# Another hand-written order of steps in a one-core attention and feed-forward layer

## The chip, the cores and the metric

The kernel runs on one core of one Trainium2 chip. The metric is the device time of an execution in microseconds (us); less is better. Five engines matter: TensorE (PE in the profile, its weight loads PEld), VectorE (DVE), ScalarE (ACT), GpSimd (POOL), and SyncE (SP), whose queue issues nearly all DMAs here. Each engine runs its own list of instructions in order. An instruction that waits holds up all that stands behind it on its engine, and a DMA that waits for its source holds up the DMAs behind it on SP's queue.

## The reference

The input x has 2048 rows of 640. There are 32 heads of 20 columns. All inputs are bfloat16.

```python
def _A_ref(x, wqkv, w_phi, wo):
    q, k, v = qkv[0], qkv[1], qkv[2]
    pq = jnp.einsum("bhsd,hdf->bhsf", q, w_phi)
    pk = jnp.einsum("bhsd,hdf->bhsf", k, w_phi)
    phi_q = jnp.concatenate([_softmax(pq, axis=-1), _softmax(-pq, axis=-1)], axis=-1)
    phi_k = jnp.concatenate([_softmax(pk, axis=-1), _softmax(-pk, axis=-1)], axis=-1)
    kv = jnp.einsum("bhsf,bhsd->bhfd", phi_k, v)
    z  = jnp.einsum("bhsf->bhf", phi_k)
    num = jnp.einsum("bhqf,bhfd->bhqd", phi_q, kv)
    den = jnp.einsum("bhqf,bhf->bhq", phi_q, z)[..., None] + 1e-6
    o = num / den
    return (lambda x, *d: x.transpose(*d))(o, 0, 2, 1, 3).reshape(B, S, D) @ wo
...
h = x + _A_ref(_layernorm(x, axis=-1), A_wqkv, A_w_phi, A_wo)
h2 = h + _B_ref(_layernorm(h, axis=-1), B_w1, B_w2)
```

`_B_ref` is a product with w1 (640 x 1728), a SiLU, and a product with w2 (1728 x 640). The layer norm has no weights. Linear attention of this kind needs the sum over all 2048 keys before any query can be finished.

## The kernel before

The rows are cut into 16 tiles of 128 (t = 0 to 15). All work is cut into named steps, `add(name, emit)`; the string `ORDER` lists the names, and at the end of the kernel one loop runs through it and emits each step's instructions:

```python
for name in ORDER:
    steps.pop(name)()
```

No scheduler comes after that. The order of the list is the order of the instructions on each engine, and so what waits behind what. The engines run beside each other: two steps that stand side by side in the list and belong to different engines overlap, as far as their inputs allow. The dictionary `ON` names the engine of those steps that can run on more than one.

The steps, by their engine and the lines of the profile:

- **Loads** stand ahead of the list and are not part of it: on SP's queue, in this order, X's first row tile (L165), five blocks of Wk (L168), X tile 1, Wv (L178), X tiles 2 and 3, Wq (L180), X tiles 4 to 7, X tiles 8 to 15. `load0` to `load11` in the list are the loads of wo (0), w1 (1 to 5), w2 (6 to 9) and the last rows of w2 (10 and 11), all on SP (L421).
- **Folding.** The products with w_phi are folded into the weights once: `wk0..4` transpose Wk on PE (L306), `wke` copies the result from PSUM (L323), `fk` multiplies it with phi on PE (L333), and `fk..e` copies it to Wfk (L342). For the queries `wq0..4` transposes Wq by DMA on SP into WTq (L325, one block each), `fq` multiplies on PE (L333), `fq..e` copies (L342). `warm` steps are matmuls on constants, `phi_a` and `phi_b` set up the folded factor on VectorE.
- **Normalising a tile:** `st` the moments on VectorE (L373, L374), `rs` the inverse deviation (on ScalarE by a logarithm and an exponential, L379 and L380; on POOL by an addition and a power, L382 and L385), `xn` the normalised row (L389, VectorE or POOL), `xt` its transposition (tiles 0 to 3 on PE, L396, with a copy `x` from PSUM, L416; the others by DMA on SP, L418).
- **Keys and values:** `K` and `V` project on PE (L429), `ex` takes the exponentials on ScalarE (L461), `su` sums them on VectorE (L465), `rk` inverts the sums on ScalarE (L473, L474), `sc` scales on VectorE (L478), `ve` copies the values on ScalarE (L482), and `kv` adds the tile into the key-value sums on PE (L497).
- **Queries:** `Q` projects on PE (L444), `qe` exponentials on ScalarE (L557), `qs` sums and `qr` ratios on VectorE (L561, L569 to L579), `qt` transposes by DMA on SP (L585).
- **Attention:** after `kv15`, `bd0` and `bd1` on VectorE mask the sums into KVB (L506, L508). `D` multiplies on PE (L610), `E` divides on VectorE (L622, L623), `ot` transposes by DMA (L634), `G` is the product with wo on PE (L643), `ga` adds the residual on VectorE (L650).
- **Feed-forward:** `ls`, `lr`, `hn`, `ht` normalise and transpose again (VectorE, POOL, VectorE, SP L670). From there tiles 0 and 1 stand alone and the others go in pairs: `u2.4` is the product with w1 of the pair that begins with tile 2, block 4 (L733; `.L` the last half block, L744), `s` its SiLU on ScalarE (L753), `lt` the transposition of the last half block (L763), `d` the product with w2 on PE (L771), `oa` the last addition on VectorE (L780) and `out` the store on SP (L785).

Two kinds of buffers tie the steps together. PSUM has eight banks: up to the step `halves` they are three pairs that go round in the order of the PE steps that take one (two more banks hold the key-value sums), after it eight single banks that go round. A PE step waits until the step that read the bank's last content is done. In SBUF there are four buffers each for the normalised rows, the key exponentials and the values, three for the transposed queries.

Of the kernel before, what the change touches and what calls it, by code (L numbers as in the profile page):

```python
# [34 lines left out]
s0.L ga20 lr1 lt0 u0.4 s0.0 hn1 qr4 G21 ht1 s0.4 u0.8 ga21 ls2 u0.12 s0.8 G30 s0.12 lr2 G31 ga30 d00
hn2 ga31 ht2 ls3 qt4 u1.L qs5 lr3 u1.0 s1.L d01 hn3 s1.0 oa00 ht3 qr5 lt1 u1.4 oa01 qs6 qt5 u1.8
s1.4 qr6 u1.12 s1.8 out0 u2.L D4 s1.12 u2.0 qs7 s2.L lt2 d10 s2.0 qs8 qt6 E40 u2.2 E41 d11 s2.2 oa10
ot4 qr7 D5 oa11 u2.4 qs9 u2.6 s2.4 E50 u2.8 s2.6 E51 ot5 u2.10 s2.8 u2.12 qt7 s2.10 D6 s2.12 G40 E60
G41 E61 d20 ga40 ot6 ga41 ls4 out1 lr4 hn4 ht4 G50 G51 d21 ga50 oa20 ga51 ls5 d30 lr5 hn5 d31 qr8
# [5 lines left out]
ga91 out5 ls9 ht8 d70 qr13 lr9 hn9 d71 oa61 ht9 out6 qt13 G100 G101 ga100 oa70 D11 oa71 u8.L u8.0
ga101 s8.L E110 u8.2 E111 s8.0 qs14 ot11 u8.4 s8.2 lt8 u8.6 qr14 s8.4 u8.8 ls10 qt14 s8.6 u8.10 lr10
s8.8 out7 hn10 u8.12 s8.10 qs15 ht10 s8.12 G110 G111 ga110 D12 d80 E120 ga111 E121 d81 ls11 ot12
oa80 lr11 d90 hn11 oa81 ht11 qr15 d91 oa90 G120 G121 ga120 oa91 u10.L D13 s10.L u10.0 lt10 E130 E131
u10.2 s10.0 ga121 ot13 ls12 u10.4 s10.2 lr12 u10.6 s10.4 hn12 u10.8 s10.6 ht12 u10.10 s10.8 out8
out9 qt15 u10.12 s10.10 D14 s10.12 G130 G131 ga130 d100 ga131 ls13 E140 lr13 d101 hn13 oa100 ht13  # L50
# [104 lines left out]

# [692 lines left out]
```

## Time and profile before

| | us |
|---|---|
| median of 3 runs | 237.06 (236.93 to 239.13) |
| span of the profiled execution, first to last instruction | 235.7 |
| time around that span: median less span | 1.4 |
| PE busy | 230.5 (98%) |
| VectorE busy | 170.0 (72%) |
| ScalarE busy | 107.8 (46%) |
| POOL busy | 46.7 (20%) |

The profiled execution has no other time of its own than the span. A sum made against the trace is made against the 235.7 us; the measured times are 1.4 us above it.

The profile shows one execution. In a timeline a line has the start, the duration, the engine, the kernel's line, the operation with its output and inputs, and in brackets how long the engine sat idle before it and what ended that. Several instructions of one line that follow each other are merged (x3). Durations of matmuls overlap; from start to start is what counts. A list of waits has the engine and line that waited, what it waited for, the total in us, how often, and the longest. A DMA's line on SP's queue is its issue; it lands later, and the landing times are given apart.

The slices of the span show at which time which engine is full: VectorE is at 9 tenths or more in most slices up to a third of the span and below that afterwards, ScalarE has work up to about 90 us, and POOL mostly up to 54 us.

### The profile page before, as it was taken

The numbers are of one execution on the slowest core, as the hardware profiler recorded it, in microseconds if no ns is written. First come the engines' busy times: TensorE is split into PE (matmuls) and PEld (weight loads), VectorE is DVE, ScalarE is ACT, GpSimd is POOL, SyncE is SP. The second block draws the span as 40 slices with busy tenths as digits, with TensorE's granted clock in tenths as the row PEclk, the third lists the DMA queues.
The fourth block names the chain that finished last, engine by engine and source line by source line (L and its number), as shares of the span: only waits on it lengthen the run. The fifth ranks groups of instructions, "written<-read, shape, count | busy, mean of one in ns | idle before, by whom it ended". The sixth has DMA issues, their size and how long they took to land.

```text
span 235.7 us, 5600 instructions
## 1 busy us (share of the span) xinstructions
PE 230.5 (98%) x2256; PEld 181.4 (77%) x2256; DVE 170.0 (72%) x355; ACT 107.8 (46%) x230; POOL 46.7 (20%) x80
## 2 busy tenths in 40 slices
PE   8899999999999999999999999999999999999995
PEld 6677777777777779798877878877877977877874
DVE  4699999899999758899669787696885544463021
ACT  3788997997888777231401501400510420421500
POOL 3117778990000011200020110011001100010000
PEclk9999999999999999999999999999999999999999
DMA  6996858499452842864431695617445193222001
GB/s 167 328 389 129 103 141 170 128 202 281 101 108 64 209 88 52 107 143 92 89 86 28 139 165 116 123 32 136 85 108 55 33 147 83 31 61 61 3 29 56
DMA packets 66697, 27.50 MB, mean 117 GB/s; under 512 B 58992, under 2 KB 65648, under 8 KB 66544
## 3 DMA queue, kind: packets, MB, share of 16 engines
q1 hardware_dynamic: 66016, 27.13, 53.2%
q8 instruction: 17, 0.28, 0.5%
q10 hardware_dynamic: 656, 0.03, 0.2%
q14 instruction: 8, 0.07, 0.1%
HBM read 10.43 MB, written 2.62 MB: 55 GB/s over the span
## 4 chain that ended last, share of the span: by engine, by line
PE 90%; DMA 6%; SPq 2%; issue 0%; DVE 0%; DVEq 0%
PE banks L733 24%; PE banks L771 24%; PE banks L429 15%; PE banks L444 9%; PE banks L643 9%; DMA Wq<-in_A_wqkv_dram 4%; DMA WTq<-Wq 3%; PE banks L497 2%; PE banks L610 2%; PE banks L774 2%; PE banks L744 1%; PE banks L333 1%; SPq L168 1%; SPq L165 1%; SPq L178 0%
## 5 line engine op out<-in xcount | busy, mean ns | idle before, releaser
L771 PE MATMUL banks<-w_sb,shT 128*128 128x320 bf16 (+2 forms) x429 | 61.3, 295 | 0.0
L733 PE MATMUL banks<-HnT,w_sb 128*128 128x256 bf16 (+1 forms) x585 | 60.0, 261 | 0.0
L733 PEld LDWEIGHTS <-w_sb 128*128 128x128 bf16 x585 | 51.3, 98 | 5.4
L771 PEld LDWEIGHTS <-shT 128*128 128x128 bf16 x429 | 41.1, 98 | 15.0
L753 ACT ACTIVATE shT<-banks 128x512 bf16<-128x512 f32 (+2 forms) x57 | 31.4, 559 | 36.0 <-PE banks L733 34.6
L429 PEld LDWEIGHTS <-XnT 128*128 128x128 bf16 x320 | 30.3, 98 | 12.0 <-issue 1.1
L382 POOL TENSOR_SCALAR rs<-mv 128x1 f32<-128x1 f32 x22 | 5.0, 227 | 159.9 <-DVE mv L374 159.8
L373 DVE BATCH_NORM_STATS2 st<-X 128x6 f32<-128x320 bf16 x64 | 27.9, 477 | 4.6 <-DMA X<-in_A_x_dram 4.5
L759 ACT ACTIVATE sh_l<-banks 128x128 bf16<-128x128 f32 x9 | 2.5, 278 | 62.4 <-PE banks L744 50.8
L780 DVE TENSOR_TENSOR o_t<-banks,X 128x320 bf16<-128x320 f32 (+2 forms) x33 | 15.5, 476 | 19.2 <-PE banks L774 19.2
L650 DVE TENSOR_TENSOR X<-banks,X 128x320 bf16<-128x320 f32 x32 | 15.3, 484 | 15.2 <-PE banks L643 15.0
L643 PE MATMUL banks<-wo_sb,OT 128*128 128x320 bf16 x160 | 25.1, 299 | 0.0
L429 PE MATMUL banks<-Wv,XnT 128*128 128x320 bf16 x160 | 23.8, 299 | 1.0 <-DMA Wv<-in_A_wqkv_dram 1.0
L557 ACT ACTIVATE EQ<-banks 128x660 bf16<-128x660 f32 (+2 forms) x48 | 21.8, 541 | 5.2 <-PE banks L444 5.0
L561 DVE TENSOR_REDUCE Sq<-EQ 128x66 f32<-128x1320 bf16 x16 | 24.2, 1516 | 0.0
L429 PE MATMUL banks<-Wfk,XnT 128*128 128x320 bf16 x160 | 24.0, 299 | 0.0
L444 PE MATMUL banks<-Wfq,XnT 128*128 128x360 bf16 (+2 forms) x160 | 23.3, 300 | 0.0
L465 DVE TENSOR_REDUCE Sk<-EK 128x64 f32<-128x1280 bf16 x16 | 23.3, 1465 | 0.0
L389 POOL TENSOR_SCALAR xn<-X,mv,rs 128x640 bf16<-128x640 bf16 x9 | 22.6, 2508 | 3.3 <-ACT rs L380 3.0
L461 ACT ACTIVATE EK<-banks 128x640 bf16<-128x640 f32 x32 | 20.7, 699 | 1.5 <-PE banks L429 1.4
L444 PEld LDWEIGHTS <-XnT 128*128 128x128 bf16 x160 | 15.4, 97 | 6.4
L643 PEld LDWEIGHTS <-OT 128*128 128x128 bf16 x160 | 15.2, 98 | 5.1
(63 smaller groups left out, 208.3 us busy)
## 6 DMA issues: line engine op xcount, KB each, us to landing
...
X<-in_A_x_dram SPq DMA_DIRECT2D x1, 1280.0 KB, 13.4
...
```

Source lines behind the costliest of these rows:

```text
L373: nc.vector.bn_stats(st[:, i, :], X[:, t, i * HD : (i + 1) * HD])
L389: eng.tensor_scalar(out=xn_[t][:], in0=X[:, t, :], scalar1=mv_.pop(t)[:, 0:1], scalar2=rs_.pop(t)[:], op0=ALU.subtract, op1=ALU.mult,)
L429: nc.tensor.matmul(ps[:, g, 0:HD], XnT[:, c, t * P : (t + 1) * P], W[:, c, g * HD : (g + 1) * HD], start=(c == 0), stop=(c == C - 1),)
L444: nc.tensor.matmul(ps[:, 0 : e - a], XnT[:, c, t * P : (t + 1) * P], Wfq[:, c, a:e], start=(c == 0), stop=(c == C - 1),)
L461: nc.scalar.activation(E5[:, :, :, b, :], p4, AF.Exp, scale=sign)
L465: nc.vector.tensor_reduce(sk[t][:], ek[t][:, 0 : H * HF].rearrange("p (q f) -> p q f", f=DH), axis=AX.X, op=ALU.add)
L557: nc.scalar.activation(features(t, a, b)[:, :, :, i], p4, AF.Exp, scale=sign)
L561: nc.vector.tensor_reduce(sq[t][:], EQ[0][:, t, :, 0:FCH].rearrange("p c (q f) -> p c q f", f=DH), axis=AX.X, op=ALU.add)
L643: nc.tensor.matmul(ps[:, 0:HD], ot[t][:, c, :], wo_sb[:, c, g * HD : (g + 1) * HD], start=(c == 0), stop=(c == C - 1),)
L733: nc.tensor.matmul(ps[:, at : at + n], w1_sb[:, c, fc * P : fc * P + P], HnT[u][:, c, 0:n], start=(c == 0), stop=(c == C - 1),)
L753: nc.scalar.activation(shT[u][:, f0 * n : f1 * n], ps_of.pop(("u", u, f0))[:, 0 : (f1 - f0) * n], AF.Silu)
L771: nc.tensor.matmul(ps[:, 0 : b - a], shT[u][:, at : at + P], w2_sb[:, fc, a:b], start=(fc == 0), stop=False,)
```

## The change

The list `ORDER` is replaced by another one with the same steps. The two are alike only at the end, from `d120` on. The order of the tiles stays, but which step of one kind stands beside which of another changes nearly everywhere: the warm matmuls all come first, the DMA transposes of Wq come in another order (`wq3 wq0 load10 wq1 wq4 load3 xt4 wq2` on SP, instead of `wq0 wq1 wq2 xt4 wq3 xt5 wq4`), the weight loads stand elsewhere, the Q steps lie differently between the key steps, and the blocks of a feed-forward pair are computed in another sequence.

`ON` moves some steps: the normalised rows on VectorE are now those of tiles 0, 2, 4, 9, 11, 12 and 14 (before: 0, 1, 2, 3, 4, 6 and 12), the other nine stay on POOL or go there; the inverse deviations on ScalarE are now those of tiles 0, 5, 7 and 14 (before ten: 0, 2, 3, 7, 8, 9, 10, 12, 14 and 15), the others are on POOL; the copy `wke3` goes from ScalarE to VectorE. What each step computes is unchanged.

```diff
--- before.py
+++ after.py
@@ -16,44 +16,42 @@
 ORDER = """
-warm5 warm2 warm15 warm7 warm20 warm13 warm0 warm16 warm18 ones2 warm9 warm8 ones3 warm6 st0 warm10
-ones1 warm12 warm19 warm17 phi_b warm21 rs0 warm1 phi_a warm4 warm3 wk0 xn0 warm11 warm14 wke0 wk1
-xt0 wk2 wke1 wk3 wke2 fk1 wke3 x0 wk4 st1 fk1e fk2 fk3 fk2e fk0 wke4 rs1 fk3e fk4 V0 ones0 fk4e xn1
-st2 fk0e xt1 K0 st3 rs2 x1 xn2 rs3 xt2 ex0 K1 xn3 x2 st4 wq0 ve0 V1 ex1 su0 rs4 wq1 V2 ve1 st5 wq2
-xt3 ve2 xn4 K2 rs5 su1 xt4 rk0 xn5 x3 fq0 ex2 wq3 sc0 K3 st6 fq0e fq1 ex3 kv0 st7 rs6 xt5 V3 pad0
-st8 rk1 wq4 fq1e K4 sc1 rs7 ve3 xn6 xn7 V4 su2 rs8 xt6 ex4 kv1 su3 V5 ve4 xn8 xt7 rk2 st9 K5 ve5 rk3
-sc2 rs9 fq2 su4 K6 ex5 zeros xt8 xn9 fq2e sc3 kv2 load0 fq3 ex6 st10 V6 pad1 xt9 su5 fq3e kv3 mask
-ve6 K7 load1 rs10 su6 rk4 xn10 V7 rk5 ex7 sc4 V8 sc5 ve7 st11 xt10 fq4 kv4 su7 fq4e rs11 kv5 K8 ve8
-xn11 rk6 st12 K9 ex8 sc6 st13 K10 ex9 mask0 xt11 st14 kv6 rk7 load2 V9 rs12 rs13 ex10 xn12 xn13 sc7
-xt12 Q0 rs14 su8 ve9 load3 kv7 eqp qe0 K11 xt13 st15 xn14 rk8 load4 su9 Q1 ex11 load5 V10 sc8 rs15
-rk9 su10 xn15 xt14 qe1 K12 qs0 load6 rk10 kv8 ve10 V11 load7 ex12 mask1 sc9 xt15 su11 K13 sc10 kv9
-rk11 V12 ve11 su12 ex13 V13 sc11 rk12 su13 ve12 kv10 K14 ve13 qr0 kv11 ex14 K15 qs1 qt0 rk13 V14
-ex15 su14 load8 Q2 ve14 qr1 rk14 V15 su15 qe2 qt1 Q3 sc12 ve15 sc13 rk15 Q4 qe3 sc14 sc15 kv12 qe4
-kv13 qs2 kv14 kv15 Q5 qr2 Q6 qe5 bd1 qt2 bd0 Q7 qe6 qs3 qe7 halves D0 Q8 E00 E01 D1 qe8 qs4 Q9 ot0
-load9 E10 Q10 qe9 load10 E11 Q11 qr3 qe10 qt3 D2 qe11 G00 E20 G01 ga00 ot1 Q12 ga01 E21 ls0 Q13 ot2
...
-ht5 oa21 oa30 G60 oa31 G61 ga60 qs10 D7 u4.L u4.0 s4.L lt4 E70 u4.2 s4.0 ga61 E71 u4.4 s4.2 qr9 ot7
-u4.6 s4.4 ls6 qt8 u4.8 s4.6 lr6 out2 u4.10 qt9 s4.8 hn6 qr10 u4.12 s4.10 qt10 s4.12 out3 ht6 G70 G71
...
-hn14 u12.12 ga150 ht14 G151 s12.12 d120 ga151 ls15 lr15 d121 oa120 hn15 ht15 d130 oa121 out12 u14.L
-oa130 u14.0 s14.L lt14 u14.2 s14.0 u14.4 s14.2 u14.6 s14.4 u14.8 s14.6 u14.10 s14.8 u14.12 s14.10
...
+warm5 warm2 warm15 warm7 warm20 warm13 warm0 warm16 warm18 warm9 warm8 warm6 warm10 warm12 warm19 warm17
+warm21 warm1 warm4 warm3 warm11 warm14 st0 ones2 wk0 wq3 phi_b phi_a wk2 rs0 wk1 wk3 wke0 wke1 xn0 wke2
+wk4 wke3 xt0 wq0 fk1 fk1e load10 st1 x0 wke4 fk2 fk2e fk0 fk3 pad1 fk3e rs1 fk4 wq1 fk4e st2 st3 fk0e
+xn1 wq4 V0 ve0 xt1 K0 x1 rs2 ones0 rs3 ex0 xn2 xt2 xn3 x2 K1 V1 st4 ex1 zeros ve1 su0 mask rk0 V2 rs4
+load3 st5 xt3 ve2 xn4 rs5 ones3 K2 st6 x3 xt4 ex2 fq0 fq0e K3 sc0 ex3 wq2 st9 fq1 st7 xn5 su1 su3 rs6
+xn6 fq1e rk1 ones1 sc1 kv0 su2 st8 rs7 V3 ve3 xt5 K4 rk3 V4 sc3 ex4 rs9 kv1 V5 ve4 xt6 rk2 ve5 su4 xn7
+sc2 st11 K5 rs8 fq2 st10 xn9 mask0 K6 ex5 fq3 st12 fq2e kv2 xt7 rk4 V6 kv3 ex6 K7 sc4 xn8 su5 st13 ve6
+fq3e rs10 fq4 xt8 xt9 xn10 ex7 load5 V7 kv4 rk5 rs11 fq4e ve7 V8 su7 K8 su6 ve8 sc5 xt10 ex8 K9 xn11 K10
+kv5 rk6 rs12 rk7 rs13 V9 sc6 load4 ex9 xn12 kv6 sc7 xn13 xt11 Q0 ex10 su8 xt13 st14 ve9 st15 su9 kv7 qe0
+rk8 rs15 K11 Q1 sc8 V10 xn15 kv8 rs14 xt12 pad0 xn14 su10 xt14 ex11 qs0 qe1 rk9 ve10 K12 sc9 V11 su11
+rk10 ex12 K13 sc10 kv9 V12 ve11 V13 load11 rk11 ex13 qs1 ve13 qr1 kv10 sc11 K14 xt15 kv11 su12 ve12
+load0 ex14 eqp K15 V14 su13 rk12 load8 qr0 ex15 su14 rk13 ve14 load6 Q2 rk14 load1 sc12 qe2 Q3 qe3 sc14
+su15 V15 rk15 kv12 ve15 sc13 Q4 kv13 qs2 kv14 load7 sc15 qr2 Q5 qe4 qt0 qe5 qs3 mask1 load2 qt1 Q6 load9
+kv15 bd1 Q7 Q8 halves qt2 bd0 qe6 D0 qe7 qs4 D1 E00 Q9 qe8 qe9 E01 E10 Q10 qe10 E11 qr3 qr4 Q11 D2 ot0
+E20 qe11 G00 G01 ot1 Q12 qt3 Q13 qe12 E21 ga00 ga01 ls0 qs6 G10 D3 lr0 hn0 ot2 ht0 qe13 Q14 ga10 G11 E30
+G20 qe14 Q15 qt4 qe15 ga11 E31 ls1 G21 u0.0 u0.4 ga20 ga21 ot3 u0.L lr1 u0.8 s0.L s0.0 G30 hn1 ls2 qr6
...
+lr5 ht4 D7 hn5 G61 ga60 E70 qr9 d31 d21 ga61 qs10 d30 oa21 oa30 ht5 oa31 qt9 u4.12 u4.0 u4.L E71 qt8 ls6
+u4.10 s4.0 ot7 u4.8 out2 s4.12 s4.L u4.4 u4.6 lr6 G70 out3 u4.2 hn6 G71 s4.6 qr11 qs13 lt4 ga71 s4.4
...
+ga151 ls15 lr15 d121 oa120 hn15 ht15 d130 oa121 out12 u14.L oa130 u14.0 s14.L lt14 u14.2 s14.0 u14.4
+s14.2 u14.6 s14.4 u14.8 s14.6 u14.10 s14.8 u14.12 s14.10 d131 s14.12 d140 oa131 out13 d141 oa140 d150
...
@@ -143,13 +141,13 @@
     ON = dict(
-        phi_b="DVE", rs0="ACT", phi_a="DVE", xn0="DVE", wke0="ACT", wke1="ACT", wke2="DVE", wke3="ACT",
-        x0="DVE", fk1e="ACT", fk2e="ACT", wke4="DVE", rs1="POOL", fk3e="DVE", fk4e="ACT", xn1="DVE",
-        fk0e="ACT", rs2="ACT", x1="ACT", xn2="DVE", rs3="ACT", xn3="DVE", x2="DVE", rs4="POOL", xn4="DVE",
-        rs5="POOL", xn5="POOL", x3="ACT", fq0e="ACT", rs6="POOL", fq1e="ACT", rs7="ACT", xn6="DVE", xn7="POOL",
-        rs8="ACT", xn8="POOL", rs9="ACT", xn9="POOL", fq2e="ACT", fq3e="ACT", rs10="ACT", xn10="POOL",
-        fq4e="ACT", rs11="POOL", xn11="POOL", rs12="ACT", rs13="POOL", xn12="DVE", xn13="POOL", rs14="ACT",
-        xn14="POOL", rs15="ACT", xn15="POOL",
+        rs0="ACT", wke0="ACT", wke1="ACT", xn0="DVE", wke2="DVE", wke3="DVE", fk1e="ACT", x0="DVE",
+        wke4="DVE", fk2e="ACT", fk3e="DVE", rs1="POOL", fk4e="ACT", fk0e="ACT", xn1="POOL", x1="ACT",
+        rs2="POOL", rs3="POOL", xn2="DVE", xn3="POOL", x2="DVE", rs4="POOL", xn4="DVE", rs5="ACT", x3="ACT",
+        fq0e="ACT", xn5="POOL", rs6="POOL", xn6="POOL", fq1e="ACT", rs7="ACT", rs9="POOL", xn7="POOL",
+        rs8="POOL", xn9="DVE", fq2e="ACT", xn8="POOL", fq3e="ACT", rs10="POOL", xn10="POOL", rs11="POOL",
+        fq4e="ACT", xn11="DVE", rs12="POOL", rs13="POOL", xn12="DVE", xn13="POOL", rs15="POOL", xn15="POOL",
+        rs14="ACT", xn14="DVE",
     )
```

The last two list lines of each kind that stand between marks are those of the second pair of feed-forward tiles and of the place from which both lists agree.

More of the change, by code (lines that the diff above doesn't have):

```diff
@@ L29 @@
-rk9 su10 xn15 xt14 qe1 K12 qs0 load6 rk10 kv8 ve10 V11 load7 ex12 mask1 sc9 xt15 su11 K13 sc10 kv9
-rk11 V12 ve11 su12 ex13 V13 sc11 rk12 su13 ve12 kv10 K14 ve13 qr0 kv11 ex14 K15 qs1 qt0 rk13 V14
-ex15 su14 load8 Q2 ve14 qr1 rk14 V15 su15 qe2 qt1 Q3 sc12 ve15 sc13 rk15 Q4 qe3 sc14 sc15 kv12 qe4
-kv13 qs2 kv14 kv15 Q5 qr2 Q6 qe5 bd1 qt2 bd0 Q7 qe6 qs3 qe7 halves D0 Q8 E00 E01 D1 qe8 qs4 Q9 ot0
-load9 E10 Q10 qe9 load10 E11 Q11 qr3 qe10 qt3 D2 qe11 G00 E20 G01 ga00 ot1 Q12 ga01 E21 ls0 Q13 ot2
-qe12 lr0 Q14 qe13 hn0 ht0 G10 qe14 D3 ga10 G11 load11 Q15 ga11 E30 E31 G20 qe15 ls1 u0.L ot3 u0.0
@@ L35 @@
[L35 to L39, printed above, removed]
@@ L40 @@
-ht5 oa21 oa30 G60 oa31 G61 ga60 qs10 D7 u4.L u4.0 s4.L lt4 E70 u4.2 s4.0 ga61 E71 u4.4 s4.2 qr9 ot7
-u4.6 s4.4 ls6 qt8 u4.8 s4.6 lr6 out2 u4.10 qt9 s4.8 hn6 qr10 u4.12 s4.10 qt10 s4.12 out3 ht6 G70 G71
-ga70 d40 ga71 ls7 lr7 D8 oa40 d41 E80 hn7 qs11 ht7 d50 E81 qr11 d51 oa41 qt11 oa50 qs12 u6.L u6.0
-ot8 s6.L oa51 u6.2 s6.0 lt6 D9 s6.2 out4 u6.4 E90 E91 u6.6 s6.4 qr12 ot9 u6.8 s6.6 qs13 qt12 G80
-s6.8 u6.10 u6.12 s6.10 D10 s6.12 G81 E100 G90 ga80 ga81 d60 ga90 ls8 E101 G91 lr8 d61 ot10 hn8 oa60
@@ L45 @@
[L45 to L50, printed above, removed]
@@ L51 @@
-d110 oa101 E141 ot14 d111 oa110 out10 u12.L u12.0 s12.L D15 s12.0 u12.2 E150 oa111 G140 s12.2 E151
-u12.4 ga140 ot15 u12.6 s12.4 out11 lt12 G141 s12.6 u12.8 ga141 ls14 u12.10 s12.8 lr14 G150 s12.10
-hn14 u12.12 ga150 ht14 G151 s12.12 d120 ga151 ls15 lr15 d121 oa120 hn15 ht15 d130 oa121 out12 u14.L
-oa130 u14.0 s14.L lt14 u14.2 s14.0 u14.4 s14.2 u14.6 s14.4 u14.8 s14.6 u14.10 s14.8 u14.12 s14.10
-d131 s14.12 d140 oa131 out13 d141 oa140 d150 oa141 out14 d151 oa150 out150 d152 oa151 out151 oa152
-out152
+warm5 warm2 warm15 warm7 warm20 warm13 warm0 warm16 warm18 warm9 warm8 warm6 warm10 warm12 warm19 warm17
@@ new lines @@
+qs7 ga30 lr2 u0.12 s0.4 ht1 G31 u1.L hn2 u1.0 u1.8 lt0 u1.12 s1.L s0.8 ga31 ls3 u1.4 s1.0 qs5 s0.12 ht2
+D4 s1.12 lr3 hn3 qr5 d01 qr7 qs8 d00 s1.4 lt1 s1.8 ht3 u2.0 E40 u2.4 E41 d10 u2.L oa00 qt5 qr8 qt6 oa01
+qs9 D5 u2.10 oa10 s2.0 s2.4 d11 u2.2 E50 qs11 ot4 out0 D6 s2.10 E51 s2.L s2.2 E60 G40 ga40 u2.8 lt2 ot5
+G41 oa11 E61 qt7 ga41 u2.12 ls4 out1 s2.8 u2.6 ot6 G50 s2.12 G51 lr4 s2.6 ga51 d20 ga50 G60 hn4 ls5 oa20
+lr5 ht4 D7 hn5 G61 ga60 E70 qr9 d31 d21 ga61 qs10 d30 oa21 oa30 ht5 oa31 qt9 u4.12 u4.0 u4.L E71 qt8 ls6
@@ new lines @@
+u4.10 s4.0 ot7 u4.8 out2 s4.12 s4.L u4.4 u4.6 lr6 G70 out3 u4.2 hn6 G71 s4.6 qr11 qs13 lt4 ga71 s4.4
+ga70 s4.10 s4.8 D8 E80 E81 ls7 lr7 D9 hn7 s4.2 d40 E90 d50 d51 E91 ht6 qr10 oa50 d41 ot8 oa40 ht7 u6.0
+qr13 qt10 u6.10 oa51 oa41 u6.2 qs15 u6.L ot9 u6.6 s6.0 u6.12 qr15 s6.L s6.10 u6.4 qs14 s6.2 s6.6 s6.4
+qr14 lt6 D10 E100 G90 qs12 u6.8 G80 out5 out4 s6.12 E101 ga90 G91 ga91 s6.8 G81 ga80 ga81 qt11 ot10 ls8
+ls9 d70 d60 lr8 d71 lr9 hn8 qr12 G100 hn9 D11 oa70 ht8 oa60 E110 E111 oa71 G101 d61 ht9 u8.2 u8.L ga100
@@ new lines @@
+u8.6 u8.0 s8.0 ga101 oa61 s8.L s8.2 out7 s8.6 ot11 u8.8 u8.12 u8.4 G110 qt12 qt13 u8.10 D12 ls10 s8.4
+G111 lt8 ga110 E120 s8.8 ga111 ls11 lr10 out6 s8.12 E121 D13 s8.10 E130 lr11 d90 hn11 d80 d91 ot12 ht11
+hn10 oa80 E131 d81 ht10 G120 oa90 G121 u10.0 ga120 qt15 ga121 u10.6 oa91 qt14 s10.0 s10.6 ot13 u10.10
+ls12 oa81 u10.L s10.L u10.4 u10.12 u10.2 u10.8 out8 G130 s10.10 lr12 s10.2 G131 out9 s10.12 D14 ga130
+lt10 s10.8 hn12 s10.4 d100 ga131 ls13 E140 d110 lr13 d111 E141 D15 ht12 d101 oa100 oa110 hn13 oa111 ht13
@@ L57 @@
+u12.0 u12.L s12.L ot14 u12.10 E150 E151 u12.12 u12.2 G140 u12.4 oa101 s12.0 s12.2 G141 s12.10 ga140 ot15
+s12.12 ga141 ls14 lt12 u12.6 u12.8 s12.4 lr14 s12.6 hn14 G150 out10 ga150 ht14 out11 G151 s12.8 d120
+ga151 ls15 lr15 d121 oa120 hn15 ht15 d130 oa121 out12 u14.L oa130 u14.0 s14.L lt14 u14.2 s14.0 u14.4
+s14.2 u14.6 s14.4 u14.8 s14.6 u14.10 s14.8 u14.12 s14.10 d131 s14.12 d140 oa131 out13 d141 oa140 d150
+oa141 out14 d151 oa150 out150 d152 oa151 out151 oa152 out152
 """.split()
```

## Prediction

> **What bounds the kernel now.** I read the page's busy table first, then what TensorE waited for, then its timeline from 9 to 24 us, then the transposes of Wq on SP's queue.
>
> ```profile
> span 235.7 us, 5600 instructions
> PE 230.5 (98%) x2256; PEld 181.4 (77%) x2256; DVE 170.0 (72%) x355; ACT 107.8 (46%) x230; POOL 46.7 (20%) x80
> ```
>
> ```profile
> PE banks L429 <- DMA Wv<-in_A_wqkv_dram: 1.0, 1, 1.0
> PE banks L231 <- PEq L832: 0.8, 1, 0.8
> PE banks L333 <- DMA WTq<-Wq: 0.3, 1, 0.3
> ```
>
> The second fence is complete: TensorE waits three times, 2.1 us in all, and never after 20.35 us. Its instructions are the same in both lists (2256 matmuls), at a granted clock of 1.00 in every slice. So little can be won. The first 0.8 us is the start; the 1.0 us ahead of V0 is Wv's landing at 10.6 us, and the loads of Wv, Wq and X stand ahead of both lists, unchanged. Only the 0.3 us at fq0 is in reach.
>
> ```profile
> 10.63 1.52 PE L429 MATMUL banks<-Wv,XnT 128*128 128x320 bf16 x10 [1.01 <-DMA Wv<-in_A_wqkv_dram]
> ...
> 18.54 1.52 PE L429 MATMUL banks<-Wfk,XnT 128*128 128x320 bf16 x10
> 20.35 0.57 PE L333 MATMUL banks<-phi,WTq 128*128 128x240 bf16 x6 [0.29 <-DMA WTq<-Wq]
> 20.76 1.52 PE L429 MATMUL banks<-Wfk,XnT 128*128 128x320 bf16 x10
> 22.11 0.56 PE L333 MATMUL banks<-phi,WTq 128*128 128x240 bf16 x6
> ```
>
> Here K2 (18.54) ends at about 20.06, fq0 starts 0.29 later, K3 and fq1 follow without a gap. fq0 needs the transposed block 0 of Wq, made by step wq0. The issues on SP, with the landing times that the trace's answer for WTq gives window by window:
>
> ```profile
> 5.11 0.43 SPq L180 DMA_DIRECT2D Wq<-in_A_wqkv_dram  x1
> ...
> 13.46 4.78 SPq L325 DMA_TRANSPOSE WTq<-Wq  x3
> 18.89 1.24 SPq L418 DMA_TRANSPOSE XnT<-xn  x1
> 20.18 1.27 SPq L325 DMA_TRANSPOSE WTq<-Wq  x1
> ```
>
> The three of 13.46 are wq0, wq1, wq2. They start at 13.46, 14.79 and 16.5 and land after 6.8, 6.1 and 4.9 us: at 20.3, 20.9 and 21.4. The last load of X (1280 KB, 13.4 us to landing) is still moving when they are issued, and they come out behind it one after the other, 0.5 to 0.6 us apart. The first in the queue is the one that PE waits for.
>
> **The change, part by part.**
>
> *Wq's transposes.* SP's old order is wq0 wq1 wq2 xt4 wq3 xt5 wq4; the new one is wq3 wq0 load10 wq1 wq4 load3 xt4 wq2 xt5. TensorE's order around it stays "xt3 K2 fq0 K3 fq1 kv0", so the first block that it needs is now second in the queue. It lands where the second landed: 14.79 + 6.1 = 20.9 instead of 20.3. V0 still starts at 10.63 with Wv, and the same steps lie between, so PE reaches fq0 at 20.1 and waits 0.9 instead of 0.3: **+0.6 us**. Bounds: wq0 lands with the first (0), or a whole issue later (1.7 us, the longest issue in that tile's rows); I take 0.6, the difference of two measured landings. fq1 needs wq1, now issued at about 17, behind a load of 80 KB; by the third's landing, 21.4, and one more place, 22.0; PE reaches it at 22.7. Hidden.
>
> *xt4 behind load3.* xt4 was issued at 18.89. Its row xn4 is done at 18.9 in the new order too (POOL has xn3 until 17.1 and then rs4), but SP is busy: 13.46 + 1.29 + 1.66 + 0.6 (load10) + 1.7 + 1.3 + 0.6 (load3) gives 20.6. The old transposes behind a load of weights landed after 2.9 to 4.3 us, so 23.5 to 24.9. PE reaches K4 at 24.21 + 0.6 = 24.8. Cost 0 to 0.2; I take **0.1**.
>
> *The head.* All 22 warm matmuls now stand ahead of wk0, and wke3 (now VectorE's) and st1 ahead of x0 on VectorE. st1 waits for X's second row, landing at 7.3, so x0 ends at about 8.9 instead of 7.6, and fk0, which takes its PSUM pair, starts at 9.0. Then fk3 and fk4 (0.4 each): PE is ready at 10.2, before Wv. xn1 moves to POOL: mv1 at 8.5, rs1 0.9 (8.73 to 9.61 in the old trace), xn1 2.5 by POOL's row L389 (VectorE's takes 0.44), so 12.0; PE wants xt1 at 11.99. 0.1 late, and xt2 about 0.1 as before. All of it falls into the 0.9 us that PE waits at fq0: nothing. Without that cover it costs 0.1 to 0.2.
>
> *Other engines.* Six inverse deviations net go from ScalarE to POOL: ScalarE loses 6 x (0.29 + 0.20) = 3.0 us, POOL gains 6 x (0.23 + 0.57) = 4.8 us. Row normalisations stay nine on POOL and seven on VectorE, but VectorE's are now 9, 11, 12, 14 instead of 1, 3, 6, 12. VectorE idles before 16 us and is 95 to 100% busy from 18 to 78, so it loses work where it had room and gains two of 0.36 us (spacing) where it has none: +0.7 us for the key stage. What covers it is the place of the Q steps. Old: "Q4 kv12 kv13 kv14 kv15 Q5 Q6 Q7 D0"; new: "kv12 Q4 kv13 kv14 Q5 Q6 kv15 Q7 Q8 D0". Adding up VectorE's queue by its rows, start to start (sums 1.39 us, scales 0.73, moments 1.02, query sums 1.44), against PE's steps laid end to end, kv13 is ready 0.5 us early, kv15 1.8 early; D0, 1.4 us later than before on PE, has one more query sum (1.44) ahead of bd1. The same addition for the old list puts sc15 at 68.6, where the trace has 68.9, so I count on 0.2 of the 0.5. G00 then waits for ot0, issued at 78.1, landing 2.6 later (OT's row), at 80.7; PE is there at 81.1. **0**, with the least cover of all at kv13 and G00.
>
> *POOL's longer queue.* Where rs of one tile stands behind xn of another, POOL holds up xt. By 2.5 us per xn, xt8 is issued at 33.2 and xt10 at 37.5; with 2.4 to 4.1 us to landing (all but the two slowest of the old list) they are there at 37.3 and 41.6 at latest, and V8 and K10 start at 38.2 and 42.3. Hidden.
>
> *ScalarE*, by its spacing of 1.18 us for a pair of exponentials and 0.58 for a copy, is due within 0.1 us of PE at K7, fq4, Q0 and K11 (PSUM pairs come free). The old list has such places too (V1 and V6, 0.2 early by the same addition), and PE did not wait there. 0, bound 0.2.
>
> *From D0 to the last four tiles* the order of feed-forward blocks and of activations is shuffled, but PE's work between a row's normalisation and its use stays long. I followed each transpose to its user: the nearest are u4.10, whose PSUM half E71 frees 0.1 us ahead (E71 stands behind oa30, which waits for d30), u6.0 and u12.0 with 0.5 to 0.7 behind ht7 and ht13 (2.4 us to landing). Weight loads end by 75 us; the first use is at 81. 0, bound 0.3 at u4.10. From d120 on both lists are equal, so the end moves with PE.
>
> **Sum.** +0.6 + 0.1 = +0.7 us. The profiled execution has a span of 235.7; I expect 236.4. The median of the three runs is 237.06, 1.4 above that span, and I keep the 1.4: 237.8.
>
> A rule of the Trainium skill speaks against more POOL work: "SBUF — State Buffer", section "Who interferes with whom", says that VectorE and GpSimd share a port pair, and that a VectorE instruction with two SBUF inputs and a GpSimd one that reads SBUF fully block each other. The trace does not show a full block:
>
> ```profile
> 30.54 2.50 POOL L389 TENSOR_SCALAR xn<-X,mv,rs 128x640 bf16<-128x640 bf16 x1 [0.18 <-ACT rs L380]
> ```
> ```profile
> 31.15 0.93 DVE L478 TENSOR_TENSOR EK<-EK,Rk 128x1280 bf16<-128x1280 bf16 x1
> ...
> 55.29 0.81 DVE L478 TENSOR_TENSOR EK<-EK,Rk 128x1280 bf16<-128x1280 bf16 x1
> ```
>
> The scale at 31.15 runs inside POOL's xn and takes 0.12 more than the one at 55.29, when POOL is idle; it does not wait until 33.04.
>
> **Rivals.**
> - *VectorE comes late in the key stage.* For: 0.2 to 0.5 us of cover at kv13, and scales of 0.77 to 1.07 us beside POOL. Against: PE never waited there before. Scales 0.12 longer throughout bring kv13 0.6 late and G00 0.3 late; with the ScalarE places up to 1.4 in all: 238.1 to 239.2. Chance 0.18.
> - *No change.* wq0 lands with the first, if the queue empties at once rather than one by one. Against: landings 0.6 apart. Then 236.8 to 237.3, at best 0.3 below the old median. Chance 0.12.
> - *Slower by over 1%: POOL's power steps hold VectorE's scales.* Six more of 0.57 us; no scale stands beside one in the old trace. If each held one scale for its length, VectorE would be 3.4 us later by kv13; it decides from 0.2 to 0.5 us on, and would cost 2.9 or more on top of 0.7: 240.7. A full block is not what the xn rows show. The skill's section above would have it so. Chance 0.08, other late transposes included (the slowest XnT landing, 6.7 us, would cost xt8 or xt10 1.5 to 2).
>
> **Numbers.** Forecast 0.62 (237.4 to 238.0). One per cent, 2.4 us, is about what a measurement of this kernel tells from no change. Faster by over 1% would need PE to be rid of more waiting than it has: 0.01. Slower by over 1%: 0.10. The range goes from no change, 237.0, through the late VectorE, 239.2.
>
> **What would show it.** fq0 waiting 0.8 to 1.0 us for WTq and starting near 20.9; K4 at most 0.2; no other wait of PE beyond 0.3; span near 236.4; scales still 0.8 to 1.0. Wrong if PE waits in the key stage (kv, D0, G00) or for XnT, or if fq0 starts at 20.3.

## The result: slower by 0.8 per cent, and the waits are not where they were forecast

| | before | after |
|---|---|---|
| median of 10 runs each, us | 237.33 (236.93 to 239.13) | 239.30 (238.49 to 240.82) |
| ratio of the times | | 1.0076, 95% interval 1.0053 to 1.0099 |
| span of the profiled execution, us | 235.7 | 238.2 |

The ratio is 1.8 us on 237.3 (1.3 to 2.3). The forecast was +0.7: right in that the change costs less than 1%, too low by 1.1 in size. As a time, 239.3 lies 0.1 above the upper end of the range, 239.2. Of the 1.5 us by which it misses 237.8, 0.3 comes from the starting point: the forecast began from 237.06, the kernel before had 237.33 in this comparison.

The head of the page of the kernel after:

```profile
span 238.2 us, 5589 instructions
...
PE 231.1 (97%) x2256; PEld 181.7 (76%) x2256; DVE 169.5 (71%) x356; ACT 103.3 (43%) x215; POOL 54.0 (23%) x92
```

TensorE has the same work (231.1 us, before 230.5). POOL has 7.3 us more, ScalarE 4.5 less, VectorE as much as before. So the loss is waiting, and the list of TensorE's waits, complete, says which (engine, buffer and line that waited, what it waited for, total us, times, longest):

```profile
PE banks L427 <- DMA Wv<-in_A_wqkv_dram: 0.8, 1, 0.8
PE banks L229 <- PEq L830: 0.8, 1, 0.8
PE banks L427 <- DMA XnT<-xn: 0.8, 1, 0.8
PE banks L331 <- DVE XnT L414: 0.7, 1, 0.7
PE banks L427 <- ACT Sk L471: 0.6, 1, 0.6
PE banks L331 <- DMA WTq<-Wq: 0.2, 1, 0.2
PE banks L394 <- DVE xn L387: 0.2, 1, 0.2
```

(Lines are two lower than in the kernel before.) The first two were there before: Wv's landing, 1.0 then, and the start. The 0.7 for XnT from VectorE lies ahead of V0, where TensorE waits for Wv anyway. What is new and counts are 0.8 for a transposed row (K4), 0.6 (K10) and 0.2 (xt2); the 0.2 at fq0 was 0.3 before. In TensorE's timeline:

```profile
11.43 1.52 PE L427 MATMUL banks<-Wv,XnT 128*128 128x320 bf16 x10 [0.84 <-DMA Wv<-in_A_wqkv_dram]
...
19.43 1.52 PE L427 MATMUL banks<-Wfk,XnT 128*128 128x320 bf16 x10
21.18 0.57 PE L331 MATMUL banks<-phi,WTq 128*128 128x240 bf16 x6 [0.23 <-DMA WTq<-Wq]
...
26.02 1.26 PE L427 MATMUL banks<-Wfk,XnT 128*128 128x320 bf16 x8 [0.81 <-DMA XnT<-xn]
...
44.29 1.53 PE L427 MATMUL banks<-Wfk,XnT 128*128 128x320 bf16 x10 [0.60 <-ACT Sk L471]
```

The line of 26.02 is K4, the last one K10. The bracket of K10 names an operation of ScalarE (of step `rk7`, 44.06 to 44.30) that ended at that moment but is not one that K10 needs; the copy that frees K10's PSUM pair, `ve8`, had ended on ScalarE at 41.70. The weight loads of the same step name the true releaser:

```profile
44.29 1.20 PEld L427 LDWEIGHTS <-XnT 128*128 128x128 bf16 x10 [0.93 <-DMA XnT<-xn]
```

So both late ones are transposes by DMA. SP's queue shows how they were issued:

```profile
14.22 3.04 SPq L323 DMA_TRANSPOSE WTq<-Wq  x2
17.30 0.60 SPq L419 DMA_DIRECT2D w_last<-in_B_w_dram  x1
17.95 3.03 SPq L323 DMA_TRANSPOSE WTq<-Wq  x2
21.02 0.58 SPq L419 DMA_DIRECT2D w_sb<-in_B_w_dram  x1
21.70 1.21 SPq L416 DMA_TRANSPOSE XnT<-xn  x1
...
37.94 0.57 SPq L419 DMA_DIRECT2D w_sb<-in_B_w_dram  x1
39.44 1.21 SPq L416 DMA_TRANSPOSE XnT<-xn  x1
```

The list of DMA issues gives the times from issue to landing, first of xt4 and then of xt10:

```profile
XnT<-xn SPq DMA_TRANSPOSE x1, 4.3
XnT<-xn SPq DMA_TRANSPOSE x1, 4.8
```

xt4 goes out at 21.70, behind four transposes of Wq and two loads, the last of 432 KB (load3), and lands 4.3 us later. xt10 goes out at 39.44, behind load5 (432 KB, 37.94), and lands after 4.8. xt10 stands that late because its row, xn10, ends on POOL at 39.41.

**V0 is 0.8 us later than in the old profile, since Wv landed later.** Wv was issued at 4.07 in both and landed after 6.5 us before, 7.3 after. Whether the new order has a part in that is taken up at the end of the experiments. To keep it apart, the following table takes every profile from V0 on. The last column adds up the waits of 0.15 us and more that TensorE's timeline shows after V0. All profiles in it are of executions at full clock; the control's was not (0.944), and is not used.

| kernel | ratio [95%] | V0 at | span | span less V0 | waits after V0 |
|---|---|---|---|---|---|
| before | 1 | 10.63 | 235.7 | 225.1 | 0.3 |
| after | 1.0076 [1.0053, 1.0099] | 11.43 | 238.2 | 226.8 | 1.9 |
| after without load3 ahead of xt4 | 1.0071 [1.0042, 1.0100] | 11.49 | 238.2 | 226.7 | 1.8 |
| after without load4, load5 there | 1.0074 [1.0041, 1.0106] | 11.49 | 237.9 | 226.4 | 1.2 |
| after without any of the three | 1.0038 [1.0008, 1.0068] | 11.55 | 237.4 | 225.9 | 1.0 |
| the same, wq0 first | 1.0037 [1.0009, 1.0066] | 11.29 | 238.1 | 226.8 | 1.3 |
| before, once more (control) | 1.0009 [0.9975, 1.0044] | | | | |
| before, wq1 first | 1.0003 [0.9970, 1.0036] | 10.80 | 235.4 | 224.6 | 0 |
| after, old engines | 1.0121 [1.0089, 1.0152] | 11.18 | 239.0 | 227.8 | 2.6 |
| before, new engines | 1.0196 [1.0162, 1.0231] | 10.72 | 240.7 | 230.0 | 4.0 |
| after, old head | 1.0064 [1.0034, 1.0094] | 11.05 | 237.6 | 226.6 | 1.7 |
| the same, without the three loads | 1.0029 [0.9997, 1.0060] | 11.30 | 237.1 | 225.8 | 0.9 |
| before, with load3 and load5 ahead | 1.0004 [0.9971, 1.0037] | 11.75 | 237.7 | 226.0 | 1.2 |
| after, mask0 later | 1.0074 [1.0038, 1.0109] | 11.36 | 237.5 | 226.1 | 1.0 |

Span less V0 less the waits is 224.6 to 225.3 in all but two (225.6 with wq0 first, 226.0 with the new engines in the old order). So from V0 on the time follows the waits of TensorE, to within 0.7 us (1.4 with those two), and before to after it grows by 1.7 us, of which the waits are 1.6. That agrees with the ratio's 1.8, with V0 left out of it.

### The profile page after: what moved, and what is told of

It is laid out like the page before. It is cut to its first block, busy times and chain, and to the rows that moved or that the text cites. A ratio compares the mean times of both kernels' runs of the same rounds, so it can differ in the third digit from the quotient of the medians.

```text
span 238.2 us, 5589 instructions
## 1 busy us (share of the span) xinstructions
PE 231.1 (97%) x2256; PEld 181.7 (76%) x2256; DVE 169.5 (71%) x356; ACT 103.3 (43%) x215; POOL 54.0 (23%) x92
## 4 chain that ended last, share of the span: by engine, by line
PE 87%; DMA 5%; DVE 4%; SPq 1%; ACT 1%; issue 0%; DVEq 0%
PE banks L731 24%; PE banks L769 24%; PE banks L427 13%; PE banks L442 9%; PE banks L641 9%; DMA X<-in_A_x_dram 3%; PE banks L608 2%; PE banks L495 2%; PE banks L772 2%; DVE st L371 2%; DMA XnT<-xn 2%; PE banks L742 1%; SPq L166 1%; DVE Sk L463 1%; ACT EK L459 1%; PE banks L331 1%
## 5 line engine op out<-in xcount | busy, mean ns | idle before, releaser
L751 ACT ACTIVATE shT<-banks 128x512 bf16<-128x512 f32 (+2 forms) x57 | 29.9, 560 | 77.8 <-PE banks L731 77.8
L731 PE MATMUL banks<-HnT,w_sb 128*128 128x256 bf16 (+1 forms) x585 | 61.0, 261 | 0.0
L380 POOL TENSOR_SCALAR rs<-mv 128x1 f32<-128x1 f32 x28 | 6.6, 236 | 156.3 <-DVE mv L372 156.2
L427 PEld LDWEIGHTS <-XnT 128*128 128x128 bf16 x320 | 30.1, 98 | 13.7 <-DMA XnT<-xn 2.1
L641 PE MATMUL banks<-wo_sb,OT 128*128 128x320 bf16 x160 | 25.6, 299 | 0.0
L387 POOL TENSOR_SCALAR xn<-X,mv,rs 128x640 bf16<-128x640 bf16 x9 | 24.0, 2663 | 1.7 <-DVE st L371 1.1
L442 PEld LDWEIGHTS <-XnT 128*128 128x128 bf16 x160 | 15.1, 97 | 6.2
L383 POOL TENSOR_TENSOR rs<-rs,nhalf_t 128x1 f32<-128x1 f32 x28 | 16.5, 589 | 2.3
```

Source lines behind the costliest of these rows:

```text
L387: eng.tensor_scalar(out=xn_[t][:], in0=X[:, t, :], scalar1=mv_.pop(t)[:, 0:1], scalar2=rs_.pop(t)[:], op0=ALU.subtract, op1=ALU.mult,)
L427: nc.tensor.matmul(ps[:, g, 0:HD], XnT[:, c, t * P : (t + 1) * P], W[:, c, g * HD : (g + 1) * HD], start=(c == 0), stop=(c == C - 1),)
L442: nc.tensor.matmul(ps[:, 0 : e - a], XnT[:, c, t * P : (t + 1) * P], Wfq[:, c, a:e], start=(c == 0), stop=(c == C - 1),)
L641: nc.tensor.matmul(ps[:, 0:HD], ot[t][:, c, :], wo_sb[:, c, g * HD : (g + 1) * HD], start=(c == 0), stop=(c == C - 1),)
L731: nc.tensor.matmul(ps[:, at : at + n], w1_sb[:, c, fc * P : fc * P + P], HnT[u][:, c, 0:n], start=(c == 0), stop=(c == C - 1),)
L751: nc.scalar.activation(shT[u][:, f0 * n : f1 * n], ps_of.pop(("u", u, f0))[:, 0 : (f1 - f0) * n], AF.Silu)
```

## The experiments

**Without load3 ahead of xt4.** The new kernel; load3 moves to a later place in the list, where VectorE masks the sums.

```diff
-V2 rs4 load3 st5 xt3 ... halves qt2 bd0
+V2 rs4 st5 xt3 ... halves qt2 load3 bd0
```

> The changed kernel with load3 taken from ahead of xt4 and put behind qt2. Theory (two transposes of normalised rows land late behind weight loads, xt4 at K4 and xt10 at K10): xt4 lands 1.5 to 2 us after the 21.70 less 0.6 of its issue plus 1.2, so before 24.5, and K4's wait of 0.8 us goes. But xt10 is due by POOL's queue and by load5, not by TensorE, so K10 then waits about 0.8 longer, 1.4 in all: time within 0.3 us of the changed kernel, ratio to the kernel before 1.006 to 1.008. Rival (the waits are separate costs that add up): 0.8 us less, ratio about 1.004. Rival (VectorE or ScalarE is late): no wait for XnT at K10 grows, and another wait appears between K4 and K10.

**Without load4 and load5 ahead of xt10 and xt11.**

```diff
-xn10 ex7 load5 V7 ... sc6 load4 ex9 ... load6 Q2 rk14 load1 sc12
+xn10 ex7 V7 ... sc6 ex9 ... load6 load5 Q2 rk14 load1 load4 sc12
```

> The changed kernel with load5 and load4, which stand ahead of xt10 and xt11, put among the late loads. Theory: xt10 lands 2.4 to 3 us after its issue at 39.4 instead of 4.8, K10's wait of 0.6 us goes, K4's of 0.8 stays: 0.6 us less than the changed kernel, ratio 1.005. Rival (POOL's queue is what makes xt10 late, the load adds nothing): K10 still waits 0.4 or more, ratio 1.007.

**Without all three.** Both edits together.

> The changed kernel with load3, load4 and load5 all moved as in the two runs before. Theory: no wait for XnT at K4 nor K10; what is left is fq0 waiting for the second transposition of Wq, 0.6 to 0.9 us: ratio 1.002 to 1.003. Rival (VectorE late in the key stage): TensorE waits at kv steps or D0 instead, ratio 1.005 or more.

**The same, with wq0 first in the queue.**

```diff
-wk0 wq3 phi_b ... xt0 wq0 fk1
+wk0 wq0 phi_b ... xt0 wq3 fk1
```

> As the run before, and with wq0 and wq3 exchanged in the list, so that the first block that TensorE needs is transposed first. Theory: fq0's wait falls back to 0.3 us or less, ratio 0.999 to 1.001, everything of the change's loss is undone by moving four DMAs. Rival (the landing of the first transposition is not what fq0 waits for): as the run before, ratio 1.002 to 1.003.

Without load3, xt4 lands 2.4 us after its issue instead of 4.3, and K4 does not wait:

```profile
XnT<-xn SPq DMA_TRANSPOSE x1, 2.4
```

But K10 waits 1.33 instead of 0.60, for xt10's time is set by POOL and the load ahead of it and not by when TensorE gets there. Without load4 and load5, K10 does not wait, and K4 waits 1.08. Only without all three do both waits go, and the ratio falls to 1.0038: the medians are 239.77 and 239.79 us with one of the two waits left and 238.83 with neither. Two waits one behind the other on the same engine: taking away one alone gained nothing that the times can tell. The three loads thus make about half of the loss. What is then late next, in TensorE's timeline of the kernel without the three loads:

```profile
28.43 1.53 PE L427 MATMUL banks<-Wv,XnT 128*128 128x320 bf16 x10 [0.35 <-DMA XnT<-xn]
61.77 0.51 PE L495 MATMUL banks<-VP,EK 128*128 128x63 bf16 x11 [0.39 <-DVE EK L476]
```

V5 waits for xt5 and kv11 for a scale of VectorE. xt5 took 4.5 us to landing there, with no load directly ahead of it, and 2.8 in the kernel after; why is not shown. In the kernel after no kv step waits; it seems that the 1.4 us lost at K4 and K10 gave VectorE the time. The theory for this run had fq0 waiting 0.6 to 0.9, and it did not wait at all. So wq0 first had nothing to undo and gained nothing (1.0037 against 1.0038); in that execution fq0 waited 0.17 although its block was the first.

**The kernel before once more, and wq1 first in it.** The first is unchanged; the second exchanges two steps.

```diff
-x2 st4 wq0 ve0 V1 ex1 su0 rs4 wq1 V2
+x2 st4 wq1 ve0 V1 ex1 su0 rs4 wq0 V2
```

> The kernel before once more, unchanged, to see what is chance. In the five profiles with the new order V0 starts at 11.3 to 11.6 us, against 10.6 in the old profile, although the loads ahead of the list are the same code. Theory: the later landing of Wv is chance of an execution or of the chip, not the order's doing; then this profile shows V0 anywhere from 10.6 to 11.6 and the ratio is 1.000, give or take 0.002. Rival: the new order makes Wv land later; then V0 starts at 10.6 here again and up to 0.8 us of the loss belongs to the head.

> The kernel before, wq0 and wq1 exchanged in the list, so that the first needed transposed block of Wq is the second in SP's queue, as in the new kernel. Theory (the prediction's term): fq0 waits about 0.9 us instead of 0.3 where V0 starts at 10.6, and less by as much as V0 starts later; ratio at most 1.0025. Rival: the blocks land together, fq0 waits 0.3 or less; ratio 1.000.

The control gives 1.0009, with an interval of 0.0035 to both sides: differences below 0.3% are not to be told from these times. With wq1 first, the term of the prediction by itself, the ratio is 1.0003, and fq0 does not wait at all, in TensorE's timeline:

```profile
20.07 0.56 PE L331 MATMUL banks<-phi,WTq 128*128 128x240 bf16 x6
```

The trace gives 5.5 us from issue to landing for the first of Wq's transposes in that execution and 4.7 for the second, against 6.8 and 6.1 in the profile before, though they were issued 0.2 us later. wq0, second, landed at about 19.7 (15.03 + 4.7), ahead of TensorE. The load that moves ahead of these transposes, X's last one, had landed at 18.6, against 19.7 in the profile before. The theory fell.

**Order and engines exchanged.** The new order with the old dictionary of engines (the diff shows five of its entries), and the old order with the new one.

```diff
-xn1="POOL", ... xn3="POOL", ... rs5="ACT", ... rs9="POOL", ... xn9="DVE",
+xn1="DVE", ... xn3="DVE", ... rs5="POOL", ... rs9="ACT", ... xn9="POOL",
```

> The new order with the old choice of engines for normalisations and inverse deviations. Theory: K4's wait of 0.8 us for XnT stays, since load3 still stands ahead of xt4; K10's wait of 0.6 goes, since POOL is no longer behind; ratio about 1.005 (1.8 us less 0.6). Rival 1: K10's wait stays, as load5 ahead of xt10 is what makes it; 1.0076 as the new kernel. Rival 2: the engines are the whole loss; 1.000 to 1.002.

> The old order with the new choice of engines. Theory: POOL's longer queue and the scales that hold it make a transposed row or two late, a wait for XnT of 0.5 to 1.5 us between K4 and K10; ratio 1.002 to 1.006. Rival: in the old order no weight load stands ahead of the transposes, so POOL's queue stays covered and PE does not wait in the key stage; 1.000.

Both are slower than the kernel after: 1.0121 and 1.0196. Neither theory had that. With the old engines in the new order, TensorE waits for xn1, which then stands on VectorE behind the moments of tiles 2 and 3, and after it for xn2:

```profile
14.44 0.45 PE L394 MATMUL banks<-ident,xn 128*128 128x128 bf16 x5 [1.74 <-DVE xn L387]
16.59 0.45 PE L394 MATMUL banks<-ident,xn 128*128 128x128 bf16 x5 [0.34 <-DVE xn L387]
```

K4 and K10 then come later and do not wait. With the new engines in the old order, the two lines that matter are one of VectorE and one of TensorE:

```profile
34.89 1.12 DVE L389 TENSOR_SCALAR xn<-X,mv,rs 128x640 bf16<-128x640 bf16 x1 [3.19 <-POOL rs L385]
...
36.79 0.51 PE L497 MATMUL banks<-VP,EK 128*128 128x63 bf16 x11 [2.02 <-DVE EK L478]
```

VectorE stands 3.19 us at a normalisation, because its inverse deviation is on POOL, behind a normalisation there that starts at 31.48 and takes 2.51; the scale behind it comes late, and TensorE waits 2.02 for it, half of its waits in the table. The old choice of engines costs the new order 1.1 us, and the new one costs the old order 4.7: each choice did worse in the other's order.

**The old head.** All steps up to V0 as before on TensorE, VectorE and ScalarE; POOL's and SP's orders stay new. Once in the kernel after, once in the one without the three loads.

```diff
-warm5 ... warm14 st0 ones2 wk0 wq3 phi_b phi_a wk2 rs0 wk1 wk3 ... wke3 xt0 wq0 fk1 fk1e load10 st1 x0 ...
+warm5 ... ones2 pad1 ... wk0 xn0 warm11 warm14 wke0 wk1 xt0 wk2 wke1 wk3 wke2 fk1 wke3 x0 wk4 st1 ... V0
```

> The new kernel with the old order of everything ahead of V0 on TensorE, VectorE and ScalarE (warm matmuls between the transposes of Wk, x0 ahead of st1); POOL's and SP's orders, the loads ahead of the transposes and all that follows V0 stay new. Theory: the new head is what makes V0 late, as x0 waits behind the moments of X's second tile; V0 starts at 10.6 to 10.8 instead of 11.2 to 11.5, and the ratio falls from 1.0076 to about 1.0045. Rival: Wv's landing sets V0 whatever the head; V0 at 11 or later, ratio 1.0076.

> The old head together with the weight loads taken from ahead of the transposes (load3, load4, load5 later, which alone gave 1.0038). Theory: the two losses add, and what is left is VectorE's lateness at kv11 (0.4 us): ratio 1.000 to 1.002. Rival: the head costs nothing; 1.004.

With the old head in the kernel after, TensorE is ready for V0 at 10.1 instead of 10.6 and waits for Wv until 11.05; without the three loads it is ready at 10.5 and waits until 11.30. So it is Wv's landing that sets V0 in these profiles, not the head. The ratios, 1.0064 and 1.0029, lie 0.0012 and 0.0009 below those with the new head, inside the uncertainty; as far as these times tell, the head costs 0.3 us or nothing.

**The old kernel with the loads ahead.**

```diff
-rs5 su1 xt4 ... st11 xt10 ... ve9 load3 kv7 ... ex11 load5 V10
+rs5 su1 load3 xt4 ... st11 load5 xt10 ... ve9 kv7 ... ex11 V10
```

> The old kernel with load3 directly ahead of xt4 and load5 directly ahead of xt10, as in the new list, and nothing else. Theory: a transpose behind a load of 432 KB lands 4.3 to 4.8 us after its issue instead of 2.4 to 3.3; xt4 is issued 0.7 later and lands near 24, PE wants it at 24.2: K4 waits 0 to 0.6; xt10 is issued at 38.4, lands at 43, K10 is due near 42.3: waits 0.7. Ratio 1.003 to 1.005. Rival: the old order's cover is long enough; 1.000.

**The kernel after with mask0 later.**

```diff
-xn9 mask0 K6 ... xn10 ex7
+xn9 K6 ... xn10 mask0 ex7
```

> The new kernel with one POOL step (mask0, 1.32 us in the new trace) moved behind xn10; load5 stays ahead of xt10. Theory: xt10 is late because POOL is, 1.9 us behind the 37.5 that the prediction had; with xn10 done 0.7 us or more earlier, xt10 is issued at 38.8 or earlier and K10's wait of 0.6 goes; ratio about 1.005. Rival 1: load5's transfer sets the landing, and K10 waits 0.6 as before; 1.0076. Rival 2: xn8, now beside the scale of 31.45, is held in mask0's place and nothing is gained.

In TensorE's timeline of the old kernel with the loads ahead:

```profile
11.75 1.52 PE L427 MATMUL banks<-Wv,XnT 128*128 128x320 bf16 x10 [1.68 <-DMA Wv<-in_A_wqkv_dram]
44.08 1.53 PE L427 MATMUL banks<-Wfk,XnT 128*128 128x320 bf16 x10 [1.21 <-DMA XnT<-xn]
```

The first line is the old order with V0 at 11.75: a late V0 comes with the old order too. The other three profiles with the old order have V0 at 10.63 to 10.80, though, and the nine with the new one at 11.05 to 11.55, 0.7 us later than the profile before on average. If the new order cost that, the ratios of those nine kernels would have to exceed what their profiles lose from V0 on by as much; they exceed it by 0.1 us on average, with -0.9 to +0.7 in single kernels. So the late V0 is chance as far as the timed runs can tell.

K4 did not wait: here xt4 stands behind three transposes and one load, went out 8.3 us after V0 (10.3 in the kernel after) and landed after 3.4. K10 waited 1.21 in this execution, xt10 landing after 5.6 behind two loads. But the timed runs, 1.0004, do not bear out a loss of that size; the profiled execution took 239.44, in a range of 237.59 to 239.84. What load5 costs the old order stays open between nothing and 0.9 us.

With mask0 later, xt10 goes out at 38.88 instead of 39.44, load5 still ahead of it, and K10 does not wait; kv11 waits 0.20. The gain in the issue is 0.56 and not 1.32, for xn8 now starts beside the scale of 31.43 and takes 2.99 instead of 2.52: the second rival in part. And xt10 landed after 3.9 there instead of 4.8, so that only 0.56 of the 1.4 us by which it was earlier are POOL's. By the profile from V0 on the kernel loses 0.7 us less, by the timed runs nothing that can be seen (1.0074, where 1.005 lies inside the interval). So K10's wait needs load5 ahead of xt10; that it needs POOL's lateness too follows from a sum in the next section, and is not shown by this run alone. Which steps of POOL were late, in the kernel after, with the scales of VectorE that were running (first POOL's timeline, then VectorE's):

```profile
20.58 3.16 POOL L387 TENSOR_SCALAR xn<-X,mv,rs 128x640 bf16<-128x640 bf16 x1 [1.07 <-DVE st L371]
...
28.18 2.52 POOL L387 TENSOR_SCALAR xn<-X,mv,rs 128x640 bf16<-128x640 bf16 x1
...
31.51 1.32 POOL L252 TENSOR_SCALAR_AFFINE_SELECT mask<-mask 128x378 f32<-128x378 f32 x1
...
35.62 1.15 POOL L383 TENSOR_TENSOR rs<-rs,nhalf_t 128x1 f32<-128x1 f32 x1
36.89 2.52 POOL L387 TENSOR_SCALAR xn<-X,mv,rs 128x640 bf16<-128x640 bf16 x1
```

```profile
20.73 0.79 DVE L476 TENSOR_TENSOR EK<-EK,Rk 128x1280 bf16<-128x1280 bf16 x1
29.37 0.77 DVE L476 TENSOR_TENSOR EK<-EK,Rk 128x1280 bf16<-128x1280 bf16 x1
31.45 0.81 DVE L476 TENSOR_TENSOR EK<-EK,Rk 128x1280 bf16<-128x1280 bf16 x1
35.57 0.78 DVE L476 TENSOR_TENSOR EK<-EK,Rk 128x1280 bf16<-128x1280 bf16 x1
```

Three POOL steps that start within 0.15 us of a scale take 0.58 to 0.64 us longer than elsewhere (2.52, 0.70 and 0.57), 1.8 in all; the scales keep their 0.8. The scale at 29.37, in the middle of an xn of POOL, disturbs neither. The other way round it happens once in this trace: a scale at 55.45, 0.21 us behind the start of a POOL step (mask1, 0.70), takes 1.13. The 1.07 ahead of the first is xn5's wait for its inverse deviation, the step rs5, which went from POOL to ScalarE and ended there at 20.5; the bracket names VectorE's older work.

## Why the prediction was right, and where it was wrong

- **The verdict** (within 1%, 0.89) came, and the reason given for it held: the work on TensorE is unchanged, nothing but waits can come, and span less V0 follows the waits in every kernel. The mechanism inside did not hold: the forecast put the loss at fq0, and it was at K4 and K10, where the prediction said it would be wrong ("if PE waits ... for XnT"). That the total stayed under 1% is in part luck: waits that were put at 0.1 or nothing came to 1.5 us more than that, the one that the sum was built on to 0.7 less, and the interval of the ratio ends at 1.0099.
- **Wq's transposes, +0.6: fell.** fq0 waited 0.23, not 0.9; wq1 first in the old kernel gave 1.0003 and no wait, wq0 first in the new one gained nothing. The step that failed is "14.79 + 6.1": it took one execution's landing time as a property of the place in the queue. The places do hold: in all thirteen profiles of the table the first block landed 0.6 to 0.7 us after X's last load, and the second 0.5 to 0.7 after the first. But X's last load landed anywhere from 18.6 to 20.4 us, 7.5 to 9.1 after V0, and TensorE came to fq0 9.3 us or more after V0. The profile before had 9.1, at the upper end; in the kernel after it was 8.5, and fq0 waited 0.23; in nine of the thirteen fq0 did not wait, whichever block came first. The 0.3 us of the old profile, the only wait "in reach", was itself of that execution: with the first block first in the queue and V0 at 11.75, in the old kernel with the loads ahead, fq0 did not wait.
- **xt4 behind load3, 0.1: mechanism right, size wrong**, 0.8 (its own terms give 0 to 0.1, where it says 0 to 0.2). Three parts of the sum moved. The issue came 10.3 us after V0 (21.70 less 11.43) where the forecast had 10.0 (20.6 less 10.63). The landing took 4.3, the upper end of its 2.9 to 4.3. And K4 was due 13.8 us after V0 instead of 14.2, since the 0.6 at fq0, which the sum used as cover, did not come. Without load3 the landing is 2.4 and the wait gone.
- **POOL's longer queue, "Hidden": wrong**, 0.6 at K10. The forecast had xt10 issued at 37.5 with K10 due at 42.3 and a landing of at most 4.1 (the old list's third slowest is 4.3); it was 39.4, due at 43.7, landing 4.8. Counted from V0, the issue is 1.1 us later than forecast, the landing 0.7 longer and K10 0.6 later: without either of the first two the 0.7 of cover would have held. The failed step is "by 2.5 us per xn": three steps held by scales, 1.8 us, and the wait of xn5 were not in it. Nor was load5 ahead of xt10 named, though the same sum had just been made for load3.
- **The head, 0: right as to its total.** fk0 waited 0.72 for x0 and xt2 0.21; the first is covered by Wv. The cover named for the second, fq0's wait, was not there, so its 0.2 counts. The old head gained 0.3 us or nothing.
- **Other engines, 0: right for the kernel as it stands**, no kv step, D0 or G00 waits in it. The "least cover of all", put at kv13 and G00, was at kv11: it waits 0.2 to 0.45 for VectorE's scale in the three kernels without the three loads and in the one with mask0 later. That the engines could be costed apart from the order was wrong: the exchange costs 1.1 us in the new order (1.0121 against 1.0076) and 4.7 in the old.
- **ScalarE 0 and D0 on 0: right.** After K10 TensorE waits nowhere.
- **The time around the span, 1.4:** in the timed runs of all kernels it is 1.7 to 1.9. The 1.4 was a median less the span of another execution.
- **The rivals.** *VectorE late*: not as a wait of the kernel after; it is what comes next. *No change*: right about fq0, not about the rest. *POOL's power steps hold VectorE's scales*: the two do hold each other, but it was mostly POOL that stood still, three times for 1.8 us in all, against 0.3 of one scale (1.13 at 55.45). It named a late xt10 beside it, which is what came. The prediction's argument against a block ("A full block is not what the xn rows show") took a scale that began 0.6 us inside a normalisation of POOL, and in that trace scales begun 0.5 to 0.6 inside one are held for 0.3 at most. The Trainium skill, "SBUF — State Buffer", section "Who interferes with whom", says that the order of issue decides which of the two stands still. The trace agrees in part: a POOL step 0.05 us behind a scale stood (0.57 to 1.15 us) and so did the scale 0.21 behind a POOL step; but the xn of 20.58 stood though it started 0.15 ahead of its scale, and a scale begun 1.2 us into an xn did not stand (29.37: 0.77 us, the xn 2.52).

The account of the profiled execution, on the forecast's span of 236.4: V0 0.8 later (Wv's landing), fq0 0.7 less, K4 0.7 more, K10 0.6, xt2 0.2, which is 238.0; measured 238.2. V0's part is not the change's. The ten runs' median span is 237.55; with 226.8 behind V0, V0 would stand at 10.8 there, and by the same subtraction in the kernel before (235.9 to 236.2 in the larger samples, less 225.1) at 10.8 to 11.1. This last step is argued from the spans, since only profiles show V0.
